# Strassen–Winograd chains of an expert layer: the second product of a chain accumulated into the first one's PSUM bank instead of added by VectorE

## The chip, the cores and the metric

One core of one Trainium2 chip. The metric is the device time of one execution in microseconds (us); less is better. Engines are called as in the profile: PE (matrix products), DVE (VectorE), ACT (ScalarE), POOL (GpSimd), SP (which issues the DMAs here).

## The reference, cut to what matters

Three stages stand one behind the other: a linear attention, a gated feed-forward layer, and a layer of eight experts, whose input `x` has 2304 tokens of 512 features. The change is in the last:

```python
logits = x @ w_gate
logits = logits - logits.max()
P = np.exp(logits)
for _ in range(8):
    P /= P.sum(1, keepdims=True) + 1e-09
    P /= P.sum(0, keepdims=True) + 1e-09
    P *= N / E
out = np.zeros((N, D), dtype=np.float32)
for e in range(E):
    h = np.maximum(x @ w1[e], 0.0)      # 512 -> 1024
    ye = h @ w2[e]                      # 1024 -> 512
    out += P[:, e:e + 1] * ye
```

## The kernel before, in words

Every float32 operand is split into a high part (H, rounded) and a low part (L, the rest), and a product is three matmuls: H·H, H·L and L·H (`mm3`, lines 86 to 88 in the profile). ACT casts the high part (L95), DVE or POOL subtracts the low part (L98).

The expert layer, which is the part from about 577 us of the span, runs over three slices `s` of 768 tokens; in each over the eight experts `e`; and in each over four **units** `p`, 96 units in all. A unit makes two of the eight 128-feature tiles of `h` for its 768 tokens, p and p+4, as one step of Strassen–Winograd: seven half-size products instead of eight, of operands that are sums of blocks. The sums of blocks of `x` (a11, a12, a22, s1 to s4) are made once for each slice, those of `w1` (B11 … T4) in the first slice for each unit: SP loads a piece of w1, ACT casts it in two pieces (768 and 1024 elements of a partition), POOL subtracts the low part of the first piece and DVE that of the second, and the result is stored; the later slices load it ready-made. Each product is 6 matmuls (two blocks of 128 rows by three) with 384 columns, 42 in a unit.

`product(x, i, *adds)` writes into one of five PSUM banks that rotate (`bufs=5`), and what is to be done with the bank stands behind it: ACT copies the first product into the SBUF tile `c` (L724), and DVE adds the others onto what lies there (L726), seven sums in a unit. With Winograd's names, the second entry c12 is a11·B11 + s2·T2, c21 is that plus s3·T3, c22 is c21 plus s1·T1, and so on: the sums hang one on the other. `h_split` (L705 to L707) then makes the two tiles of `h`: ACT the ReLU, rounded (hH), and DVE the low part (hL). Behind a unit w2 is split (`split_w2`: ACT casts 1024 elements, POOL or DVE subtracts), two units' worth of w2 rows each.

After the fourth unit of an expert follows **the py phase**: six output tiles of 128 tokens, each 24 matmuls with 512 columns that take the eight tiles of h and w2, and DVE scales and adds the result to the output tile (L834). Between products and between pairs of py matmuls, `between()` issues one step of the normalisation of P (lines 763 to 773, "Sinkhorn"), until its 16 half steps are done; until then py tiles are copied out unscaled and wait.

The order on each engine is made by the tile framework: instructions keep the program's order with priorities, `tc.high_priority(60)` puts what empties a PSUM bank ahead. The two py banks, the five product banks and the one bank of the Sinkhorn sums are used together. A new product that takes a bank waits until its last reader is done.

Of the kernel before, what the change touches and what calls it, by code (L numbers as in the profile page):

```python
# [8 lines left out]
F32 = mybir.dt.float32  # L9
# [3 lines left out]
ENG = dict(  # L13
    kh="aaav", num="a", xmul="gvgg", xh="a", xl="ggvg", woh="a",
    wol="g", w3h="a", w3l="g", w34="aaav", wh="vvvvvvav", wl="v", oh="va", ol="vvvg", Xh="a",
    Xl="v", Xs="g", Wt="v", Wh="a", Wl="gv", W2h="a", W2l="vg",
)
AF = mybir.ActivationFunctionType
ALU = mybir.AluOpType
# [3 lines left out]
def f32(ap):  # L23
    return ap.bitcast(F32)
# [3 lines left out]
def kernel(  # L28
# [17 lines left out]
    nc = tc.nc  # L46
    PSUM = bass.MemoryType.PSUM
    P = 128
# [15 lines left out]
    N1 = 384  # L64
# [13 lines left out]
    def x_at(p, kt, c0, n):  # L78
        i, o = divmod(c0, NH)
        return XHL[i][p][:, kt, o : o + n]  # L80
# [4 lines left out]
    def mm3(ps, aH, aL, bH, bL, start, stop):  # L85
        nc.tensor.matmul(ps, aH, bH, start=start, stop=False)  # L86
        nc.tensor.matmul(ps, aH, bL, start=False, stop=False)  # L87
        nc.tensor.matmul(ps, aL, bH, start=False, stop=stop)  # L88

    def engine(key, i=0):  # L90
        return {"a": nc.scalar, "v": nc.vector, "g": nc.gpsimd}[ENG[key][i % len(ENG[key])]]
# [22 lines left out]
    with ExitStack() as c1:  # L114
# [267 lines left out]
        for n in range(3 * FT):  # L382
            s = 5 * n // 3
            w, name, i = (wo_load, f"wo{n}", n) if n < FT else (w3_load, f"w3_{n - FT}", n - FT)
# [17 lines left out]
        for step in range(NB + 8):  # L402
# [5 lines left out]
            i = step - 4  # L408
# [17 lines left out]
    c4 = ctx.enter_context(ExitStack())  # L426

    NP = FT2 // 2
# [3 lines left out]
    def add(key, out, a, b, op, i=0):  # L432
        engine(key, i).tensor_tensor(out, a, b, op)
# [61 lines left out]
    def sbuf(c, name, bufs=1, side="right"):  # L495
        return c.enter_context(tc.tile_pool(name=name, bufs=bufs, side=side, reuse_waits="tile"))
# [30 lines left out]
    with ExitStack() as c2:  # L527
# [76 lines left out]
        for j in range(NT // N1):  # L604
            c0 = j * N1
            for ft in range(FT):
                ab = []
                for w in range(2):
                    n = 2 * ft + w
# [7 lines left out]
                    ps = ab_p.tile([P, N1], F32, name=f"ab{j}_{ft}_{w}", tag="ab")  # L617
# [26 lines left out]
            for dt in range(KT):  # L644
                ps = px_p.tile([P, N1], F32, name=f"px{j}_{dt}", tag="px")
# [6 lines left out]
                i, o = divmod(c0, 2 * N1)  # L652
                nc.sync.dma_start(XS[i][:, dt, o : o + N1], xt)
                xh, xl = x_at(0, dt, c0, N1), x_at(1, dt, c0, N1)
# [19 lines left out]
    with c4:  # L674
# [3 lines left out]
        sk = sbuf(c4, "sk", 2)  # L678
        st = sbuf(c4, "st", 2)
        wp = sbuf(c4, "wp")  # L680
        ph_p = c4.enter_context(tc.tile_pool(name="ph", reuse_waits="tile", bufs=5, space=PSUM))
        py_p = c4.enter_context(tc.tile_pool(name="py", reuse_waits="tile", bufs=2, space=PSUM))
        W2, rawW2 = {}, {}
        hH = [hp.tile([P, 2 * N1], F32R, name=f"hH{i}") for i in range(FT2)]
# [20 lines left out]
        def h_split(ft, src):  # L705
            nc.scalar.activation(hH[ft], src, AF.Relu)  # L706
            nc.vector.scalar_tensor_tensor(hL[ft], src, 0.0, f32(hH[ft]), ALU.max, ALU.subtract)  # L707

        def unit(u, between):
            s, e, p = units[u]  # L710
            c = ut.tile([P, 4, N1], F32, name=f"c{u}", tag="c")
            c11, c21, c12, c22 = (c[:, i] for i in range(4))
            B11, B21, B22, T1, T2, T3, T4 = range(7)

            def product(x, i, *adds):
                ps = ph_p.tile([P, N1], F32, name=f"p{x}{u}", tag="ph")
                (wh, wl), (xh, xl) = WC[u], XC[x]
                for kt in range(2):
                    k = slice(kt * P, (kt + 1) * P)
                    mm3(ps, wh[:, i, k], wl[:, i, k], xh[:, kt], xl[:, kt], kt == 0, kt == 1)  # L720
                with tc.high_priority(60):
                    for o, t in adds:
                        if t is None:
                            nc.scalar.copy(o, ps)  # L724
                        else:
                            nc.vector.tensor_tensor(o, t, ps, ALU.add)  # L726
                between()

            product("a11", B11, (c11, None))
            product("s2", T2, (c12, c11))  # L730
            product("s3", T3, (c21, c12))
            product("s1", T1, (c22, c21), (c12, c12))
            product("a12", B21, (c11, c11))
            product("a22", T4, (c21, c21))
            h_split(p, c[:, 0:2].rearrange("p a n -> p (a n)"))
            product("s4", B22, (c12, c12))
            h_split(p + NP, c[:, 2:4].rearrange("p a n -> p (a n)"))

        m1 = sk.tile([P, 1], F32, name="m1", tag="m1", bufs=1)
        m2 = sk.tile([1, 1], F32, name="m2", tag="m2", bufs=1)  # L740
# [44 lines left out]
        def between():  # L785
            if todo:
                todo.pop()()
# [3 lines left out]
        for u, (s, e, p) in enumerate(units):  # L791
# [7 lines left out]
            if u + 2 >= len(W1S):  # L799
                prep_w1(u + 2)  # L800
            unit(u, between)
            split_w2(u)
            load_w2(u + 2)
# [6 lines left out]
            for tt in range(2 * N1 // P):  # L810
                t = s * 2 * N1 // P + tt
                ps = py_p.tile([P, DM], F32, name=f"py{e}_{t}", tag="py")
# [3 lines left out]
                o = oacc[tt]  # L816
# [96 lines left out]
```

## Time and profile before

| | us |
|---|---|
| median of 3 runs | 2124.03 (2122.5 to 2124.05) |
| profiled execution, its span | 2119.5 |
| PE busy | 2064.6 (97%) |
| DVE busy | 1155.2 (55%) |
| ACT busy | 600.5 (28%) |
| POOL busy | 348.2 (16%) |

The profiled execution is one execution; its span is the time from its first to its last recorded instruction, 4.5 us below the median. Busy time is the time in which at least one recorded instruction of the engine runs. Times of rows count from the start of the span. A row of the trace has the start, the duration of one instruction, the engine, the line, and output and inputs by the program's names; in square brackets stands how long the engine idled before it, and what it then waited for. Consecutive instructions of an engine overlap a little in the records, so that the distance of two starts is the better measure of what an instruction takes of its engine.

### The profile page before, as it was taken

Reading aid. Unit: us, or ns where it says so; the run is one execution under the profiler, and the core shown is the slowest. Engines: PE = TensorE matmul, PEld = TensorE weight load, DVE = VectorE, ACT = ScalarE, POOL = GpSimd, SP = SyncE. Lnnn points to the kernel's source line nnn. Section 1 sums busy time; section 2 is a strip of 40 time slices with the busy share of each in tenths; the row PEclk is TensorE's granted clock in tenths of the full one; section 3 lists DMA queues with packets and bytes.
Section 4 is the critical chain, followed back from the end, with each engine's and each line's share of the span. In section 5 each row is a group of like instructions: output and inputs, shape, how many; then the busy total and the mean of one; then the engine's idle time right before and its main releaser. Section 6 shows DMA issues by size and latency. Waiting matters only on the chain.

```text
span 2119.5 us, 28336 instructions
## 1 busy us (share of the span) xinstructions
PE 2064.6 (97%) x11621; PEld 1843.6 (87%) x11621; DVE 1155.2 (55%) x1766; ACT 600.5 (28%) x947; POOL 348.2 (16%) x204
## 2 busy tenths in 40 slices
PE   8899889999889999999999999999999999999999
PEld 6677789999878888888888999888999888999887
DVE  8876863333486556665555554444565444555443
ACT  6665432222332222332231221111232111122111
POOL 2432221121422211221120000000010000000000
PEclk9999999999989999999999999999999999999999
DMA  6432244555474556645564443334444334444330
GB/s 210 136 128 84 103 147 139 167 174 161 159 292 150 195 218 238 231 182 188 184 243 169 179 179 135 118 130 155 179 184 170 135 108 151 177 179 166 127 120 30
DMA packets 78529, 345.40 MB, mean 163 GB/s; under 512 B 7488, under 2 KB 11456, under 8 KB 65728
## 3 DMA queue, kind: packets, MB, share of 16 engines
q1 hardware_dynamic: 77808, 342.95, 45.0%
q8 instruction: 91, 1.49, 0.3%
q10 hardware_dynamic: 592, 0.66, 0.1%
q14 instruction: 38, 0.31, 0.0%
HBM read 256.54 MB, written 87.03 MB: 162 GB/s over the span
## 4 chain that ended last, share of the span: by engine, by line
PE 82%; DVE 8%; issue 3%; DMA 2%; ACT 2%; POOL 1%; SPq 0%; ACTq 0%; DVEq 0%; POOLq 0%
PE py L88 12%; PE py L87 12%; PE py L86 12%; PE ps L86 5%; PE ps L88 5%; PE ps L87 5%; PE pa L86 4%; PE pa L88 4%; PE pa L87 4%; PE ab L88 3%; PE ab L86 3%; PE ab L87 3%; PE nu L268 1%; PE px L86 1%; PE px L87 1%
## 5 line engine op out<-in xcount | busy, mean ns | idle before, releaser
L88 PE MATMUL py<-w2h,hL 128*128 128x512 f32 x1152 | 457.2, 397 | 0.3 <-DVE hL L707 0.2
L86 PE MATMUL py<-w2h,hH 128*128 128x512 f32 x1152 | 456.8, 397 | 0.5 <-DVE o L832 0.5
L87 PE MATMUL py<-w2l,hH 128*128 128x512 f32 x1152 | 456.9, 397 | 0.0
L834 DVE SCALAR_TENSOR_TENSOR o<-py,Pw,o 128x512 f32<-128x512 f32 x126 | 94.6, 751 | 450.9 <-PE py L88 450.9
L726 DVE TENSOR_TENSOR c<-c,ps 128x384 f32<-128x384 f32 x480 | 256.1, 549 | 90.5 <-PE ps L88 84.8
L98 POOL TENSOR_TENSOR w2l<-r,w2h 128x1024 fp32r<-128x1024 f32 x48 | 116.4, 2425 | 1108.2 <-ACT w2h L95 1081.4
L95 ACT CAST w2h<-r 128x1024 fp32r<-128x1024 f32 x96 | 101.0, 1052 | 692.1 <-PE py L88 611.9
L88 PEld LDWEIGHTS py<-w2h,hL 128*128 128x128 f32 x1152 | 216.8, 188 | 55.5 <-DVE hL L707 3.3
L86 PEld LDWEIGHTS py<-w2h,hH 128*128 128x128 f32 x1152 | 217.0, 188 | 52.6 <-DVE o L832 0.8
L87 PEld LDWEIGHTS py<-w2l,hH 128*128 128x128 f32 x1152 | 217.0, 188 | 51.5
L707 DVE SCALAR_TENSOR_TENSOR hL<-c,hH 128x768 fp32r<-128x768 f32 x192 | 234.1, 1236 | 24.5 <-ACT hH L706 22.5
L706 ACT ACTIVATE hH<-c 128x768 fp32r<-128x768 f32 x192 | 158.3, 843 | 298.3 <-DVE c L726 276.3
L86 PE MATMUL ab<-XH,wH 128*128 128x384 f32 x384 | 131.5, 343 | 6.9 <-DVE wH L95 5.4
L88 PE MATMUL ab<-XH,wL 128*128 128x384 f32 x384 | 131.1, 342 | 0.6 <-DVE wL L98 0.5
L87 PE MATMUL ab<-XL,wH 128*128 128x384 f32 x384 | 130.7, 340 | 0.0
L726 DVE TENSOR_TENSOR c<-c,pa 128x384 f32<-128x384 f32 x192 | 102.4, 549 | 16.7 <-PE pa L88 15.2
L628 POOL TENSOR_TENSOR cL<-a,cH 128x384 fp32r<-128x384 f32 x48 | 58.9, 1229 | 232.2 <-ACT cH L627 232.1
L98 DVE TENSOR_TENSOR w2l<-r,w2h 128x1024 fp32r<-128x1024 f32 x48 | 59.0, 1229 | 53.8 <-ACT w2h L95 53.8
L95 ACT CAST w<-r 128x768 fp32r<-128x768 f32 x64 | 59.6, 938 | 101.0 <-DMA r<-in_moe_w_dram 30.5
L98 POOL TENSOR_TENSOR w<-r,w 128x768 fp32r<-128x768 f32 x32 | 66.6, 2082 | 130.0 <-ACT w L95 118.0
L626 DVE TENSOR_TENSOR a<-ab,a 128x384 f32<-128x384 f32 x48 | 26.7, 557 | 109.4 <-PE ab L88 109.4
L86 PEld LDWEIGHTS ab<-XH,wH 128*128 128x128 f32 x384 | 72.9, 190 | 8.3 <-DVE wH L95 4.7
(169 smaller groups left out, 3891.5 us busy)
## 6 DMA issues: line engine op xcount, KB each, us to landing
w<-w1s SPq DMA_DIRECT2D x64, 1792.0 KB, 7.6
w1s<-w SPq DMA_DIRECT2D x32, 1792.0 KB, 6.7
r<-in_moe_w_dram SPq DMA_DIRECT2D x96, 512.0 KB, 3.4
rw<-in_w_dram SPq DMA_DIRECT2D x32, 512.0 KB, 3.5
tr<-in_moe_w_dram SPq DMA_DIRECT2D x32, 512.0 KB, 4.2
w1t<-tt SPq DMA_DIRECT2D x32, 512.0 KB, 5.1
r<-w1t SPq DMA_DIRECT2D x32, 512.0 KB, 8.1
r<-in_moe_w_dram SPq DMA_DIRECT2D x32, 384.0 KB, 7.4
```

The costliest lines, as they stand in the source:

```text
L86: nc.tensor.matmul(ps, aH, bH, start=start, stop=False)
L87: nc.tensor.matmul(ps, aH, bL, start=False, stop=False)
L88: nc.tensor.matmul(ps, aL, bH, start=False, stop=stop)
L95: (e.copy if e is nc.scalar else e.tensor_copy)(out, src)
L98: engine(key, i).tensor_tensor(out, a, b, ALU.subtract)
L268: nc.tensor.matmul(o, kv[:, hh, sg, :], eq[:, sg, hh, c], start=sg == 0, stop=sg == 1)
L626: behind = nc.vector.tensor_tensor(cc, ab[1], a_sb, ALU.mult).ins
L628: nc.gpsimd.tensor_tensor(l, cc, f32(h), ALU.subtract)
L706: nc.scalar.activation(hH[ft], src, AF.Relu)
L707: nc.vector.scalar_tensor_tensor(hL[ft], src, 0.0, f32(hH[ft]), ALU.max, ALU.subtract)
L726: nc.vector.tensor_tensor(o, t, ps, ALU.add)
L834: nc.vector.scalar_tensor_tensor(o, ps, Pw[:, t, e : e + 1], o, ALU.mult, ALU.add)
```

## The change

The banks of the products are no longer five that rotate, but four with names of their own, one bank each: p16, p53, p74 and p2 (`bufs=1`, a tag for each). The order of the products is now a11 (p16), s1 (p53), s3 (p74), s2 (p16, added by PE onto a11's product, which ACT has copied to c11 before), a12 (p2), s4 (p53, onto s1's) and a22 (p74, onto s3's). ACT copies four times in a unit (`kept`, L734), DVE adds four times (`added`, L739), and POOL adds c12 to c22 in SBUF (`add("Ht", …)`, L433, 128x384). The matmuls of products stand in L726 of the new kernel. `h_split` of tile p+4 comes ahead of that of tile p. Nothing else is edited.

```diff
-        ph_p = c4.enter_context(tc.tile_pool(name="ph", reuse_waits="tile", bufs=5, space=PSUM))
+        ph_p = c4.enter_context(tc.tile_pool(name="ph", reuse_waits="tile", bufs=1, space=PSUM))
...
-            def product(x, i, *adds):
-                ps = ph_p.tile([P, N1], F32, name=f"p{x}{u}", tag="ph")
+            bank = {}
+
+            def product(k, x, i):
+                start = k not in bank
+                if start:
+                    bank[k] = ph_p.tile([P, N1], F32, name=f"{k}{u}", tag=k)
+                ps = bank[k]
...
+                        nc.tensor.matmul(
+                            ps, w[:, i, kc], m[:, kt], start=start and kt == n == 0,
+                            stop=kt == 1 and n == 2, skip_group_check=True,
+                        )
...
-            product("a11", B11, (c11, None))
-            product("s2", T2, (c12, c11))
-            product("s3", T3, (c21, c12))
-            product("s1", T1, (c22, c21), (c12, c12))
-            product("a12", B21, (c11, c11))
-            product("a22", T4, (c21, c21))
+            kept(c11, product("p16", "a11", B11))
+            kept(c22, product("p53", "s1", T1))
+            kept(c12, product("p74", "s3", T3))
+            add("Ht", c22, c22, c12, ALU.add)
+            u2 = product("p16", "s2", T2)
+            kept(c21, u2)
+            added(c11, c11, product("p2", "a12", B21))
+            between()
+            added(c22, c22, u2)
+            added(c12, c21, product("p53", "s4", B22))
+            between()
+            h_split(p + NP, c[:, 2:4].rearrange("p a n -> p (a n)"))
+            added(c21, c21, product("p74", "a22", T4))
+            between()
             h_split(p, c[:, 0:2].rearrange("p a n -> p (a n)"))
-            product("s4", B22, (c12, c12))
-            h_split(p + NP, c[:, 2:4].rearrange("p a n -> p (a n)"))
```

What this does to the order of three engines. In the rows below a name's number is that of the tile; w_26 is the w1 piece of unit 26.

DVE in the first slice, between the sums of unit 24 and those of unit 25 (the first and second unit of an expert), before:

```order
L707 SCALAR_TENSOR_TENSOR hL_5672<-c_8619,hH_5664 128x768
L726 TENSOR_TENSOR c_8696<-c_8696,ps_8705 128x384
L707 SCALAR_TENSOR_TENSOR hL_5676<-c_8619,hH_5668 128x768
L726 TENSOR_TENSOR c_8696<-c_8696,ps_8713 128x384
L98 TENSOR_TENSOR w_26_8687<-r_26_8616,w_26_8687 128x1024
L726 TENSOR_TENSOR c_8696<-c_8696,ps_8721 128x384 x2
L726 TENSOR_TENSOR c_8696<-c_8696,pa_8730 128x384
L726 TENSOR_TENSOR c_8696<-c_8696,pa_8738 128x384
L726 TENSOR_TENSOR c_8696<-c_8696,ps_8748 128x384
```

and with the change, with the numbers of units in the names (p1625 is bank p16 of unit 25):

```order
L707 SCALAR_TENSOR_TENSOR hL4_5676<-c24_8571,hH4_5668 128x768
L707 SCALAR_TENSOR_TENSOR hL0_5672<-c24_8571,hH0_5664 128x768
L98 TENSOR_TENSOR w1_26_8637<-r1_26_8568,w1_26_8637 128x1024
L739 TENSOR_TENSOR c25_8646<-c25_8646,p1625_8647 128x384
L739 TENSOR_TENSOR c25_8646<-c25_8646,p225_8679 128x384
L739 TENSOR_TENSOR c25_8646<-c25_8646,p5325_8655 128x384
L739 TENSOR_TENSOR c25_8646<-c25_8646,p7425_8663 128x384
```

The first two sums of the next unit stood between the two hL and the w1 subtraction; now both hL and the subtraction stand ahead of all four, and the first sum is the one that frees p16.

POOL around the same place, before:

```order
L98 TENSOR_TENSOR w_25_8610<-r_25_8383,w_25_8610 128x768
L98 TENSOR_TENSOR w2l_8759<-r_25_8452,w2h_8758 128x1024
L98 TENSOR_TENSOR w2l_8913<-r_27_8762,w2h_8912 128x1024
L98 TENSOR_TENSOR w_26_8687<-r_26_8616,w_26_8687 128x768
L98 TENSOR_TENSOR w_27_8764<-r_27_8693,w_27_8764 128x768
```

and with the change:

```order
L98 TENSOR_TENSOR w2l_8707<-r_25_8404,w2h_8706 128x1024
L433 TENSOR_TENSOR c_8571<-c_8571 128x384
L98 TENSOR_TENSOR w2l_8857<-r_27_8710,w2h_8856 128x1024
L98 TENSOR_TENSOR w_26_8637<-r_26_8568,w_26_8637 128x768
L433 TENSOR_TENSOR c_8646<-c_8646 128x384
L98 TENSOR_TENSOR w_27_8712<-r_27_8643,w_27_8712 128x768
```

POOL's new addition of a unit (c_8571 is unit 24's, c_8646 unit 25's) stands behind w2 and w1 subtractions that belong to other units.

PE at the end of the gated layer, where the logits of the last tokens (`lg`, then `lp`) and the first expert's first product meet, before:

```order
L590 MATMUL lg_5618<-XH_69,WG 16x384
L591 MATMUL lg_5618<-XL_70,WG 16x384
L595 MATMUL lp<-ident,lgs_5627 128x16 x3
L86 MATMUL pa_5696<-a11h_5460,w_0_5492 128x384
L87 MATMUL pa_5696<-a11l_5461,w_0_5492 128x384
```

and with the change, behind the matmuls of the products a11, s1 and s3:

```order
L726 MATMUL p_5696<-s2h_5470,w_0_5492 128x384
L726 MATMUL p_5696<-s2l_5471,w_0_5492 128x384
L726 MATMUL p_5696<-s2h_5470,w_0_5492 128x384 x2
L726 MATMUL p_5696<-s2l_5471,w_0_5492 128x384
L726 MATMUL p_5696<-s2h_5470,w_0_5492 128x384
L726 MATMUL p_5746<-a12h_5479,w_0_5492 128x384
L726 MATMUL p_5746<-a12l_5480,w_0_5492 128x384
L726 MATMUL p_5746<-a12h_5479,w_0_5492 128x384
L590 MATMUL lg_5618<-XH_69,WG 16x384
```

27 matmuls of products (four products of six, and three of a12) now stand ahead of the last L590 of the logits. Farther on, the third py tile stands behind 220 matmuls of products and 48 of py, where it stood behind 249 and 48.

## Rows read from the trace of the kernel before

**Rows 1.** The page, its first part: busy time of each engine.
```profile
PE 2064.6 (97%) x11621; PEld 1843.6 (87%) x11621; DVE 1155.2 (55%) x1766; ACT 600.5 (28%) x947; POOL 348.2 (16%) x204
```

**Rows 2.** Busy time by stretch: first slice from its third expert, the later slices.
```profile
core 0: us, PE busy (x) PEld busy (x) DVE busy (x) ACT busy (x) POOL busy (x), PEclk, DMA share, GB/s
...
727.30:1109.30 382.00, 380.39 (x1874) 336.59 (x1873) 223.22 (x293) 116.42 (x148) 81.68 (x38) 1.00 0.57 209
1109.30:2115.60 1006.30, 1006.26 (x4993) 900.03 (x4991) 489.47 (x711) 200.08 (x262) 81.17 (x34) 1.00 0.40 147
```

**Rows 3.** Timeline of PE, first matmuls of units: start us, duration us, engine, line.
```profile
727.30 0.33 PE L86 MATMUL pa<-a11h,w 128*128 128x384 f32 x1
...
918.60 0.34 PE L86 MATMUL pa<-a11h,w 128*128 128x384 f32 x1
...
925.91 0.33 PE L86 MATMUL pa<-a11h,w 128*128 128x384 f32 x1
...
933.19 0.33 PE L86 MATMUL pa<-a11h,w 128*128 128x384 f32 x1
...
940.83 0.33 PE L86 MATMUL pa<-a11h,w 128*128 128x384 f32 x1
...
1109.27 0.34 PE L86 MATMUL pa<-a11h,w 128*128 128x384 f32 x1
...
2052.51 0.34 PE L86 MATMUL pa<-a11h,w 128*128 128x384 f32 x1
```

**Rows 4.** Groups of instructions by line: count | busy us, mean ns of one.
```profile
L726 DVE TENSOR_TENSOR c<-c,ps 128x384 f32<-128x384 f32 x480 | 256.1, 549 | 90.5 <-PE ps L88 84.8
...
L98 POOL TENSOR_TENSOR w<-r,w 128x768 fp32r<-128x768 f32 x32 | 66.6, 2082 | 130.0 <-ACT w L95 118.0 <-DVE c L726 6.3 <-DMA r<-in_moe_w_dram 5.7
...
L98 DVE TENSOR_TENSOR w<-r,w 128x1024 fp32r<-128x1024 f32 x32 | 40.4, 1262 | 17.7 <-ACT w L95 17.6
```

**Rows 5.** The gated layer's POOL subtraction: duration ns, least/median/most.
```profile
L628 POOL TENSOR_TENSOR cL<-a,cH x48: 1006/1024/5785, 258.5 to 559.4; 128x384 fp32r<-128x384 f32 x48
```

**Rows 6.** Timelines of ACT, POOL and DVE behind an expert's first unit.
```profile
924.93 1.05 ACT L95 CAST w2h<-r 128x1024 fp32r<-128x1024 f32 x1 [2.89 <-DMA r<-in_moe_w_dram]
925.88 0.85 ACT L706 ACTIVATE hH<-c 128x768 fp32r<-128x768 f32 x1
926.63 0.81 ACT L95 CAST w<-r 128x768 fp32r<-128x768 f32 x1
927.35 0.47 ACT L724 COPY c<-pa 128x384 f32<-128x384 f32 x1
927.72 0.85 ACT L706 ACTIVATE hH<-c 128x768 fp32r<-128x768 f32 x1
...
926.06 2.41 POOL L98 TENSOR_TENSOR w2l<-r,w2h 128x1024 fp32r<-128x1024 f32 x1 [4.43 <-ACT w2h L95]
928.42 2.57 POOL L98 TENSOR_TENSOR w<-r,w 128x768 fp32r<-128x768 f32 x1
...
926.76 2.52 DVE L707 SCALAR_TENSOR_TENSOR hL<-c,hH 128x768 fp32r<-128x768 f32 x1
929.20 0.54 DVE L726 TENSOR_TENSOR c<-c,ps 128x384 f32<-128x384 f32 x1
929.67 2.13 DVE L707 SCALAR_TENSOR_TENSOR hL<-c,hH 128x768 fp32r<-128x768 f32 x1
```

**Rows 7.** Timeline of PE where the expert layer starts.
```profile
585.87 0.50 PE L590 MATMUL lg<-XH,WG 128*16 128x384 f32 x1 [8.56 <-ACT XH L655]
...
588.03 0.69 PE L86 MATMUL pa<-a11h,w 128*128 128x384 f32 x1
...
599.72 0.29 PE L770 MATMUL cs<-Pw,ones 128*128 128x144 f32 x1
...
643.92 0.36 PE L770 MATMUL cs<-Pw,ones 128*128 128x144 f32 x1
...
649.18 0.36 PE L770 MATMUL cs<-Pw,ones 128*128 128x144 f32 x1
...
654.82 0.50 PE L86 MATMUL py<-w2h,hH 128*128 128x512 f32 x1 [0.47 <-DVE o L832]
```

## What the change will do to the time, forecast before it was run

> **What bounds the kernel now.** I read the page's first part first. PE is busy for 97% of the span, DVE for 55%, ACT and POOL far less [rows 1], so a change that touches DVE, ACT and POOL can gain only where PE waits for one of them. Where that is, the view of busy time by stretch tells: in the two later slices PE is busy for 1006.26 of 1006.30 us, in the first slice, from its third expert on, for 380.39 of 382.00 [rows 2]. The timeline of PE sharpens it. Sixteen experts less the last lie between 1109.27 and 2052.51, so one takes 943.24 / 15 = 62.88 us; an undisturbed unit takes 933.19 - 925.91 = 7.28, and what is left for the py phase is 62.88 - 4 x 7.28 = 33.76 [rows 3]. That is PE's own pace: 7.28 / 42 = 0.173 us for a matmul of a product and 33.76 / 144 = 0.234 for one of py. The six experts from 727.30 to 1109.27 take 63.66 each, 0.78 more; 0.36 of that is in the third unit (940.83 - 933.19 = 7.64) [rows 3], the rest in py. So in the first slice the chain of other engines' work, which there includes the split of w1, already touches PE's pace, and in the later ones nothing does. The third place is the start of the expert layer, where PE idles 8.56 us for the last logits, and the Sinkhorn steps then decide when the third py tile may start [rows 7].
>
> **What is removed, and what it is worth.** Three of seven DVE sums a unit go: 3 x 549 ns, 1.65 us of a unit of 7.28 [rows 4]. PE's matmuls stay 42 a unit, since the additions on a bank cost no matmul of their own. In the later slices DVE is busy for 489 of 1006 us [rows 2]; the sums lie beside PE's work, and their removal is worth nothing there.
>
> **What is added.** Three ACT copies a unit (starts 0.37 us apart, 927.72 - 927.35 [rows 6]) and one POOL addition of 384 elements of a partition in SBUF. That addition has no row before; the nearest is POOL's subtraction of the same size, 1.01 us at least and 5.79 at most [rows 5]. I take 1.0 and keep the upper end for the rivals.
>
> **The later slices: zero.** The banks now have fixed owners, so each one's next use may wait. By PE's pace, s2 ends at 4.16 us of a unit, its copy and its sum (0.37 and 0.55) by about 5.4, and p16 is wanted again at 7.28: 1.9 us to spare. For p53 s4 ends at 6.24, its sum at 6.9, and it is wanted at 8.32; for p74 it is 7.28, 7.9 and 9.36: 1.4 us each. What covers these is that nothing else long is on DVE then; were the cover gone, PE would wait by what is missing, in all 64 units.
>
> **The first slice.** Here the split of w1 stands between. The rows show that long DVE and POOL instructions on SBUF data exclude one another, and the first to come goes first: hL at 926.76 takes 2.52 us and ends at 929.28, 0.81 after POOL's w2 subtraction (928.47); POOL's next one starts at 928.42 and takes 2.57, ending 1.71 after hL; and the next hL (929.67, 2.13) again ends 0.81 after that. The sum from PSUM between them takes its ordinary 0.54 [rows 6]. The Trainium skill (Perfetto Trace Analysis, Optimizing Scalar/DVE Operations) says that GPSIMD and DVE share an SBUF read port and that moving work between the two might not help; the trace agrees, hL 2.52 instead of some 0.8, and by that rule too POOL's new addition costs DVE what it takes.
>
> In the new order both hL and the w1 subtraction of DVE stand ahead of all four sums of the next unit, and the first of these, onto c22, also needs POOL's addition and frees p16. I walk that through in us from an expert's first matmul (918.60), with what one takes from [rows 6]: ACT's starts 0.95 apart for a cast of 1024, 0.75 for hH, 0.72 for the cast of 768, 0.37 for a copy; hL 0.81 to 0.9, POOL's w1 piece 1.7 to 1.8, DVE's w1 piece 1.1 (1.26 in the mean, which holds waits [rows 4]), a sum 0.47 to 0.55. The w2 cast comes at 6.33 (924.93, as its DMA lands) and ends at 7.38. Then ACT: hH to 8.1, cast to 8.85, copy of c11, hH to 9.95, copy of c22, cast to 11.3, copy of c12 to 11.65. POOL subtracts w2 from 7.4 to 9.8; the first hL is held and ends at 10.65; POOL's w1 piece follows to 12.35, the second hL to 13.2, POOL's addition to 14.2, DVE's w1 piece to 15.3, and the first sum of the second unit to 15.8. The third unit wants p16 at 14.56. **PE waits 1.25 us.** Queued behind the late sum on DVE are the other three sums, which free p2, p53 and p74, and with them hH, and the next hL.
>
> After that the ring of one unit is hL 0.9 + POOL's w1 piece 1.8 + hL 0.9 + addition 1.0 + DVE's w1 1.1 + four sums 1.9 + 0.35 until hH is there = 7.95 us, 0.67 over PE's 7.28. With the sum that frees p16 the fourth unit starts 0.8 late again: it starts at 23.95 instead of 21.84, so the units lose 2.1. One ring more brings the last hL to 37.15. The first py tile wants it at 31.2 + 18 x 0.234 + 0.5 = 35.9, so py loses 1.25. Together **3.3 us an expert, where 0.78 is lost now: 2.5 more.** The last expert of the slice splits w1 in two units only, so the 0.8 of its fourth unit falls away: 1.7 more. In the second expert half of the units' 2.1 counts, 1.1, as PE waits for Sinkhorn there in any case; the first has no earlier unit to carry. Sum: 5 x 2.5 + 1.7 + 1.1 = +15.4. The bounds: nothing, if the ring stays under 7.28, and about +31, if POOL's addition takes twice as much in this crowd.
>
> **The start.** 27 product matmuls move into the wait of 8.56 us, and the third py tile has 29 fewer product matmuls ahead of it (220 for 249), which are left for later: 29 x 0.173 = 5.0 us more behind it. When can it start? Before, at 654.82, which is 5.64 after the last of eight Sinkhorn sums; seven distances between these fill 599.72 to 649.18, 7.07 each, and the last is 5.26 [rows 7]. If the distances stay at 7.07, nothing moves and the change costs 5.0. If all are 5.26, the tile starts 12.7 earlier, and it gains 7.6. With three DVE sums fewer between the steps I take 5.8: 8.9 earlier, **-3.8** net.
>
> **Sum.** 15.4 - 3.8 = +11.6. The profiled execution would have a span of 2119.5 + 11.6 = 2131.1; the median stands 4.5 above that execution, so 2135.6.
>
> **Rivals.**
> Faster: the ring is shorter than PE's unit. If POOL's w1 piece (1.8 of the 7.95) ran beside the four sums, which pass POOL unharmed [rows 6], the ring would be 6.15 and the first slice would lose even its 0.78 x 6 = 4.7 of now; with the start's -3.8 it gives 2115.5. The point is whether ACT's cast of 768 ends before DVE's first hL begins. For it speaks that DVE has 1.65 us less to do; against it that the cast stands behind hH in ACT's order, and that hH releases hL too. I give it 0.17.
>
> No difference: the ring fits, but the first stall of each expert remains in part, as the w2 subtraction of POOL comes at the same time whatever the ring does. Half a microsecond more for seven experts, 3.5, and -3.8 from the start: 2123.7. For it speaks that before, with an equally long list, the third unit lost only 0.36 [rows 3]. I give it 0.18.
>
> Much slower: the four single banks hold PE in every unit, in the later slices too. At 0.3 us a unit it is 64 x 0.3 = 19 more, 2155. The spare 1.4 to 1.9 us speak against it; 0.07. The Trainium skill (Perfetto Trace Analysis, Matmuls) asks that independent groups of matmuls rotate through different PSUM banks, so that the emptying of one overlaps the next; by it this change is the wrong way round. No row before shows the banks as the limit.
>
> The clock is one more price in the slower cases: right behind the idle 8.56 us a product's matmul takes 0.69 in its row and not 0.33 [rows 3, 7]; were PE to idle that long again, it would count twice. The stalls above are of one microsecond, so I count nothing for it. That the change doesn't do what it says can be left out: the order has four sums and 42 matmuls in a unit.
>
> **How the numbers follow.** The forecast, slower by more than 0.2% (4.2 us, about what a measurement of this kernel can tell from no change), gets 0.58, with its own range from 2128 to 2150 (the start's bounds, and the stalls at about half and at one and a half of their size). With the rivals: slower 0.58 + 0.07 = 0.65, same 0.18, faster 0.17. The range leaves out the much slower case and the better part of the faster one, 0.07 + 0.12: 2117 to 2150.
>
> **What would show it.** Right, if the six middle experts of the first slice take some 66 us instead of 63.66, if the late matmul there is the first of the third and fourth units and waits for the sum onto c22 behind DVE's w1 piece, if the last hL holds the first py tile, and if the sixteen later experts stay at 62.88. In the start the distances of the Sinkhorn sums should be near 5.8. Wrong, if the units of the first slice take 7.28 with POOL's addition in place, or if a later slice's unit takes more than 7.28.

## The result, and the profile after

The changed kernel takes 2145.98 us (median of 4 runs, 2141.11 to 2147.45), the kernel before 2124.04 (4 runs, 2122.5 to 2125.57): a ratio of 1.0101, 95% interval 1.0087 to 1.0115, 22 us slower. The forecast was 2135.6 in a range of 2117 to 2150.

The first part of the page and the groups of DVE, ACT and POOL in the changed kernel, which answer to [rows 1, 4, 5]:

```profile
PE 2072.8 (97%) x11621; PEld 1846.7 (86%) x11621; DVE 1037.7 (48%) x1478; ACT 728.4 (34%) x1235; POOL 479.9 (22%) x300
...
L739 DVE TENSOR_TENSOR c<-c,p 128x384 f32<-128x384 f32 x384 | 200.0, 550 | 163.4 <-POOL c L433 116.2
...
L707 DVE SCALAR_TENSOR_TENSOR hL<-c,hH 128x768 fp32r<-128x768 f32 x192 | 240.8, 1265 | 29.6 <-ACT hH L706 27.4
L706 ACT ACTIVATE hH<-c 128x768 fp32r<-128x768 f32 x192 | 160.6, 845 | 211.4 <-DVE c L739 195.3
L734 ACT COPY c<-p 128x384 f32<-128x384 f32 x384 | 181.0, 478 | 119.6 <-PE p L726 119.0
L433 POOL TENSOR_TENSOR c<-c 128x384 f32<-128x384 f32 x96 | 132.8, 1384 | 272.9 <-ACT c L734 272.9
```

DVE is busy for 118 us less and the kernel is 22 us slower. The sums now wait: of their 163 us of idle time before them 116 end with POOL's new addition, which takes 1.38 us in the mean.

The timeline of PE in the changed kernel: the logits matmul ahead of the wait, the third py tile, first matmuls of experts and of late units, two late py matmuls, and the first matmul of the last expert:

```profile
580.99 0.35 PE L591 MATMUL lg<-XL,WG 128*16 128x384 f32 x1
...
650.27 0.50 PE L86 MATMUL py<-w2h,hH 128*128 128x512 f32 x1
...
730.96 0.34 PE L726 MATMUL p<-a11h,w 128*128 128x384 f32 x1
...
945.37 0.44 PE L726 MATMUL p<-a11h,w 128*128 128x384 f32 x1 [1.00 <-DVE c L739]
953.29 0.44 PE L726 MATMUL p<-a11h,w 128*128 128x384 f32 x1 [0.34 <-DVE c L739]
966.54 0.50 PE L88 MATMUL py<-w2h,hL 128*128 128x512 f32 x1 [0.99 <-DVE hL L707]
...
1061.59 0.34 PE L726 MATMUL p<-a11h,w 128*128 128x384 f32 x1
1132.65 0.34 PE L726 MATMUL p<-a11h,w 128*128 128x384 f32 x1
1609.33 0.50 PE L88 MATMUL py<-w2h,hL 128*128 128x512 f32 x1 [2.40 <-DVE hL L707]
...
2078.66 0.34 PE L726 MATMUL p<-a11h,w 128*128 128x384 f32 x1
```

In the kernel before, the matmul that answers to the first of these, and the first matmul of the eighth expert, which answers to the one at 1061.59:

```profile
576.96 0.35 PE L591 MATMUL lg<-XL,WG 128*16 128x384 f32 x1
...
1045.61 0.34 PE L86 MATMUL pa<-a11h,w 128*128 128x384 f32 x1
```

**Where the 26.2 us between the two profiled executions (2145.7 and 2119.5) lie.** The logits matmul stands 4.0 later already (580.99 against 576.96), by code that the change does not touch, so that is one execution against another; 22.2 are the change's, which is what the medians show. From there to the third expert it is -0.4 (730.96 - 727.30 = 3.66, less 4.03). The five experts from there to the eighth take 330.63 instead of 318.31: +12.3. The eighth, the last of the first slice, takes 71.06 instead of 63.66: +7.4. The sixteen later ones, by the distance of 1132.65 to the last expert's start at 2078.66 (946.0 for 943.2), lose 2.8, which is the wait at 1609.33, at the second change of slice. That is 22.1.

The windows of the same two stretches as [rows 2]:

```profile
730.96:1132.65 401.69, 386.57 (x1873) 340.27 (x1872) 205.11 (x221) 143.63 (x220) 124.66 (x62) 0.99 0.54 199
1132.65:2142.00 1009.35, 1006.66 (x4993) 899.98 (x4991) 393.68 (x519) 290.78 (x454) 161.69 (x98) 1.00 0.40 147
```

PE waits 15.1 us in the first slice's six experts, where it waited 1.6, and in the later slices 2.7, at one place. Inside a unit the lateness runs as in the forecast. DVE and POOL in the changed kernel behind the first unit of the expert at 929.65:

```profile
937.92 4.98 DVE L707 SCALAR_TENSOR_TENSOR hL<-c,hH 128x768 fp32r<-128x768 f32 x2 [0.24 <-ACT hH L706]
942.83 2.03 DVE L98 TENSOR_TENSOR w<-r,w 128x1024 fp32r<-128x1024 f32 x1
944.78 2.12 DVE L739 TENSOR_TENSOR c<-c,p 128x384 f32<-128x384 f32 x4
...
937.15 2.41 POOL L98 TENSOR_TENSOR w2l<-r,w2h 128x1024 fp32r<-128x1024 f32 x1 [1.66 <-PE p L726]
939.52 2.57 POOL L98 TENSOR_TENSOR w<-r,w 128x768 fp32r<-128x768 f32 x1
942.04 1.73 POOL L433 TENSOR_TENSOR c<-c 128x384 f32<-128x384 f32 x1
```

The two hL take 4.98 us together, because POOL's w2 and w1 subtractions stand between them; the w1 subtraction of DVE takes 2.03 beside POOL's addition; the first sum ends at 945.3, and PE's third unit starts at 945.37.

### The profile page after: what moved, and what is told of

It reads as the page before. It is cut to its first block, busy times and chain, and to the rows that moved or that the text cites. A ratio compares the mean times of both kernels' runs of the same rounds, so it can differ in the third digit from the quotient of the medians.

```text
span 2145.7 us, 28206 instructions
## 1 busy us (share of the span) xinstructions
PE 2072.8 (97%) x11621; PEld 1846.7 (86%) x11621; DVE 1037.7 (48%) x1478; ACT 728.4 (34%) x1235; POOL 479.9 (22%) x300
## 4 chain that ended last, share of the span: by engine, by line
PE 73%; DVE 9%; issue 8%; ACT 4%; POOL 4%; DMA 3%; SPq 0%; ACTq 0%; POOLq 0%; DVEq 0%
PE p L726 23%; PE py L88 11%; PE py L86 11%; PE py L87 11%; PE ab L88 3%; PE ab L86 3%; PE ab L87 3%; DMA r<-in_moe_w_dram 2%; DVE hL L707 1%; PE nu L268 1%; PE px L88 1%; PE px L87 1%; PE px L86 1%; POOL c L433 1%; PE pp L164 1%
## 5 line engine op out<-in xcount | busy, mean ns | idle before, releaser
L739 DVE TENSOR_TENSOR c<-c,p 128x384 f32<-128x384 f32 x384 | 200.0, 550 | 163.4 <-POOL c L433 116.2
L707 DVE SCALAR_TENSOR_TENSOR hL<-c,hH 128x768 fp32r<-128x768 f32 x192 | 240.8, 1265 | 29.6 <-ACT hH L706 27.4
L734 ACT COPY c<-p 128x384 f32<-128x384 f32 x384 | 181.0, 478 | 119.6 <-PE p L726 119.0
L433 POOL TENSOR_TENSOR c<-c 128x384 f32<-128x384 f32 x96 | 132.8, 1384 | 272.9 <-ACT c L734 272.9
L726 PE MATMUL p<-a11h,w 128*128 128x384 f32 x384 | 115.0, 340 | 10.3 <-DVE c L739 10.3
L726 PE MATMUL p<-s1h,w 128*128 128x384 f32 x384 | 114.0, 337 | 0.7 <-DVE c L739 0.7
L726 PE MATMUL p<-s4h,w 128*128 128x384 f32 x384 | 113.9, 337 | 0.0
L726 PE MATMUL p<-s3h,w 128*128 128x384 f32 x384 | 113.7, 336 | 0.0
```

Source lines behind the costliest of these rows:

```text
L726: nc.tensor.matmul(ps, w[:, i, kc], m[:, kt], start=start and kt == n == 0, stop=kt == 1 and n == 2, skip_group_check=True,)
```

## The experiments

**The addition on DVE** (`ht_dve`).

```diff
-    ..., Ht="g",
+    ..., Ht="v",
```

> Only the engine of the addition c22 += c12 is changed, from POOL to DVE; it still reads two SBUF operands. Theory A (POOL's addition shuts out DVE and is shut out by it, in the chain to the sum that frees p16): about 0.5 us on DVE takes the place of 1.0 us on POOL in the ring of the first slice, 7.95 becomes 7.45, so the late starts of the third and fourth unit fall from 1.1 and 0.5 us to under half, and the time by 8 to 14 us, to 2132 to 2138. Theory B (four single banks are too few, whoever adds): the same stalls, 2144 to 2148. Theory C (ACT's three more copies make everything late): 2144 to 2148 too.

2140.32 us, ratio 1.0079 (1.0062 to 1.0096): 5.7 us less than the change, in the direction of theory A but short of its 8 to 14. The stretch of six experts, PE's wait for the third unit, and the two engines ahead of it:

```profile
730.89:1124.64 393.75, 384.21 (x1874) 338.63 (x1872) 212.54 (x245) 143.08 (x220) 82.00 (x38) 0.99 0.56 203
...
940.88 0.44 PE L726 MATMUL p<-a11h,w 128*128 128x384 f32 x1 [1.10 <-DVE c L739]
...
934.92 2.57 POOL L98 TENSOR_TENSOR w<-r,w 128x768 fp32r<-128x768 f32 x1
...
933.26 5.04 DVE L707 SCALAR_TENSOR_TENSOR hL<-c,hH 128x768 fp32r<-128x768 f32 x2 [0.16 <-ACT hH L706]
```

The fourth unit's wait and most of the py wait are gone, the third unit's is not: the two hL still take 5.04 us between POOL's w2 and w1 work. So the addition is a part of the ring, and not what holds the first one.

**The sum straight from bank p74** (`sum_psum`).

```diff
-            kept(c12, product("p74", "s3", T3))
-            add("Ht", c22, c22, c12, ALU.add)
+            added(c22, c22, product("p74", "s3", T3))
+            between()
```

> The addition in SBUF and ACT's copy of s3's product are left out; DVE adds s3's product to c22 straight from bank p74 (five sums from PSUM a unit, three copies, no POOL). Theory A: no addition on the shared port is left, the ring of the first slice is 7.95 - 1.0 + 0.5 = 7.45 at most and less where the sum passes POOL's work; units of the first slice near 7.28 to 7.5, slice changes free of their 2.5 us, 2118 to 2128. Theory B: banks as before it, 2140 to 2148. Theory C: one of three added copies gone, 2138 to 2142.

2134.29 us, ratio 1.0046 (1.0029 to 1.0063): 11.7 less than the change and outside the range of A, between A and B. The six experts take 390.91:

```profile
729.47:1120.38 390.91, 382.84 (x1873) 336.52 (x1872) 211.21 (x245) 134.11 (x196) 81.71 (x38) 1.00 0.56 205
```

POOL's 82 us of w1 and w2 work are the same as in the run before, and half the loss is still there.

**Bank p16 doubled** (`two_p16`).

```diff
-                    bank[k] = ph_p.tile([P, N1], F32, name=f"{k}{u}", tag=k)
+                    bank[k] = ph_p.tile([P, N1], F32, name=f"{k}{u}", tag=k, bufs=2 if k == "p16" else 1)
```

> Bank p16 doubled (five product banks again), all else as in the change. Theory A: the chain of sums is late as a whole, so PE then waits for p53 (wanted 1.04 us after p16, summed 0.9 later) and the last hL of an expert still comes 1.2 us late: 2141 to 2148. Theory B: the stalls at the first product of a unit vanish, 2124 to 2132.

2151.67 us, ratio 1.013 (1.0115 to 1.0145): above even A's range, and B falls. The wait only goes to the next bank, s1's p53:

```profile
950.12 0.44 PE L726 MATMUL p<-s1h,w 128*128 128x384 f32 x1 [0.87 <-DVE c L739]
958.04 0.44 PE L726 MATMUL p<-s1h,w 128*128 128x384 f32 x1 [0.34 <-DVE c L739]
970.35 0.50 PE L88 MATMUL py<-w2h,hL 128*128 128x512 f32 x1 [1.12 <-DVE hL L707]
```

Its six middle experts take 401.03 us, no more than the change's 401.69; the 5.7 us that it is slower by lie at the start. Its first matmul of a product comes at 588.20, 13.5 us after the last px matmul, as in the kernel before (13.6), which also has five product banks; in the change it comes 2.7 us after. By the start of the third expert `two_p16` is 7.1 us behind the change, counted from the last px matmul of each. Why the fifth bank holds the first products back was not tested.

**Both w1 subtractions on DVE** (`w1_dve`).

```diff
-    ..., Wl="gv", ...
+    ..., Wl="v", ...
```

> Both pieces of w1's low part are subtracted by DVE; POOL keeps the new addition and its half of w2. Theory A: POOL's 1.8 us leaves the ring and 0.85 us of DVE comes in, 7.95 becomes 7.0, under PE's 7.28: the fourth unit starts on time, the last hL too, and only the third unit is late where POOL has w2: 2128 to 2136. Theory B: 2144 to 2148. Theory C: 2144 to 2148.

2123.44 us, ratio 0.9997 (0.9987 to 1.0006, 10 runs): 22.5 less than the change, more than A expected; B and C fall. DVE gets more work and the kernel is faster. What is left of the ring (one turn of the second and third unit):

```profile
719.18:1108.35 389.17, 383.95 (x1873) 337.75 (x1872) 202.54 (x243) 143.22 (x220) 75.70 (x40) 1.00 0.56 206
...
931.67 1.67 POOL L433 TENSOR_TENSOR c<-c 128x384 f32<-128x384 f32 x1 [6.98 <-ACT c L734]
...
933.37 2.14 DVE L739 TENSOR_TENSOR c<-c,p 128x384 f32<-128x384 f32 x4 [0.90 <-POOL c L433]
```

Its units take 7.69 and not the 7.0 of the expectation: POOL's addition is held by DVE and then holds the sums for 0.9 us a turn.

**The same move in the kernel before** (`before_w1_dve`), the same edit of one letter.

> The kernel before with both w1 subtractions on DVE, which took 22 us off the changed kernel. Theory A (the exclusion of DVE and POOL costs where the order has no spare time behind it; before, five rotating banks and sums between the two hL carried it): little is there to gain, its units lose 0.36 us only, and DVE makes three sums more: 2118 to 2126. Rival D (POOL's w1 piece is simply a bad place, in either kernel): the kernel before gains as much, 2102 to 2110.

2114.98 us, ratio 0.996 (0.9945 to 0.9975): 8.4 less than before: 3 under A's range and 5 above D's, so neither held as written. POOL's w1 piece costs the kernel before 8, and the changed one 22.

**All of w2 on DVE** (`w2_dve`).

```diff
-    ..., W2l="vg", ...
+    ..., W2l="v", ...
```

> The change with all w2 low parts on DVE; POOL keeps w1's first piece and the addition. Theory A: an expert's first ring loses POOL's 2.4 us of w2, so its third unit starts on time (7.3 to 7.5 instead of 8.3 to 8.45), while the fourth unit, behind the ring of 7.95, stays at 7.9 or takes what the third lost (up to 8.3): 2135 to 2142. Theory B' (the addition on POOL alone holds the third unit): third unit as before it, 2143 to 2148.

2137.68 us, ratio 1.0065 (1.005 to 1.008): in A's range. The fourth unit's first matmul still waits, the third's is nearly on time:

```profile
934.60 0.44 PE L726 MATMUL p<-a11h,w 128*128 128x384 f32 x1
...
942.52 0.44 PE L726 MATMUL p<-a11h,w 128*128 128x384 f32 x1 [0.34 <-DVE c L739]
```

In this expert the third unit starts 7.53 after the second and the fourth 7.92 after the third, 8.44 and 7.92 in the change. The first wait is the w2 subtraction's, the second the ring's, as expected.

**w1 on DVE and the sum from PSUM** (`w1_psum`), the edits of `w1_dve` and `sum_psum` together.

> Two edits together: c22's addition taken from bank p74 by DVE (no copy, no POOL), and both w1 subtractions on DVE; POOL keeps half of w2. Theory A: no ring over 7.28 is left, first-slice experts 62.9 to 63.3 instead of 66 and instead of 64.0 with w1 alone; the two slice changes still lose some 2 and 4; with the start's gain of about 5 us 2113 to 2120. Rival B (single banks hold what remains): experts near 64, 2121 to 2126.

2112.22 us, ratio 0.9949 (0.9932 to 0.9965), a little under the range; six experts in 381.25 us, 0.75 less than before. B falls here a second time: the four banks are as in the change.

**The sums of blocks of x on DVE** (`x_dve`).

```diff
-    ..., Xs="g", ...
+    ..., Xs="v", ...
```

> The change with one edit: the sums of blocks of x (made once a slice) on DVE; the w1 and w2 parts and the new addition stay on POOL. Theory A (exclusion of DVE and POOL, here at the start and at the two slice changes): the slice changes lose 1 to 3 us each instead of 4.6 and 2.8, the idle stretch of PE before the last logits gets shorter, the middle experts stay at 66: 2132 to 2140. Rival E (DVE's own list ahead of the last hL is what is late at a slice change): 2143 to 2149, the slice changes as in the change.

2130.49 us, ratio 1.0034 (1.0021 to 1.0047): 15.5 less than the change, more than A expected; E falls. The middle experts stay at 66, as expected. The last expert of the first slice takes 65.53 (71.06 in the change), the one ahead of the second change of slice 62.94 (65.65), and at the start the last logits matmul goes on without the long wait:

```profile
578.43 0.35 PE L590 MATMUL lg<-XH,WG 128*16 128x384 f32 x1
...
579.02 0.35 PE L591 MATMUL lg<-XL,WG 128*16 128x384 f32 x1
```

In the change the same step came at 589.68, and before at 585.87 [rows 7]. What held it is in the changed kernel's ACT timeline: a cast waits 3.40 us for POOL's sum, and the copies of the last px tiles stand behind it on ACT. The last copy then waits for a store (`xs<-xt`) of an earlier one, which was issued at 577.46 and landed at 588.53; in `x_dve`, where two of the last four copies come ahead of the cast and not one, the store that its last copy waits for had landed at 571.99. The kernel before has the same two waits (3.40 and 8.86 us), so they are old.

```profile
575.81 0.84 ACT L95 CAST s4h<-xs 128x768 fp32r<-128x768 f32 x1 [3.40 <-POOL xs L433]
...
576.96 0.47 ACT L651 COPY xt<-px 128x384 f32<-128x384 f32 x1
...
588.61 0.48 ACT L651 COPY xt<-px 128x384 f32<-128x384 f32 x1 [3.61 <-DMA xs<-xt]
```

From the last px matmul to the third expert it is 146.6 us, 152.5 in the change: with the two changes of slice (5.5 and 2.7) these 5.9 make up 14 of the 15.5.

**The change as it was made, with w1, w2 and the x sums on DVE** (`change_w12x`): three settings, nothing else.

> The change as it was made, with its addition on POOL and its four copies, and only the w1 and w2 parts and the sums of x moved to DVE: POOL has nothing but the addition. Theory A: the ring without POOL's w1 piece is about 7.0, PE's own pace in the first slice but for 0 to 0.4 us an expert: 2100 to 2108. Theory B'' (the addition on POOL costs the chain its 1.0 us and its exclusion wherever it stands): experts of the first slice 64 and more, 2108 to 2118.

2104.01 us, ratio 0.991 (0.9895 to 0.9924), 42 less than the change. Six experts in 380.19 us, 63.4 each: near PE's pace, with the copies, the four banks and POOL's addition all in place. That ends B and C: what made the change slower is neither the banks nor ACT's copies.

**The kernel before with the same three settings** (`before_w12x`).

> The kernel before with w1, w2 and the sums of x on DVE, that is the three engine moves of the fastest kernel so far without anything of the change. Theory A (the change's sums and banks are sound, POOL beside them is not; seven DVE sums a unit beside all the splits are too much for DVE): 2104 to 2112, 4 to 12 slower than 2099.8. Rival D (the engine moves are the whole gain, the change is worth nothing): 2098 to 2102.

2104.08 us, ratio 0.9911 (0.9897 to 0.9926), at the lower end of A's range and 2 above D's. With POOL's old work out of the way the change as made is worth nothing, 2104.0 against 2104.1. That is a small gain and a small loss: from the last px matmul to the fourth expert it takes 199.6 us where this kernel takes 201.4, and its experts in the rest of the first slice take 63.3 to 63.8 where this kernel's take 62.89.

**The sum from PSUM and all three moves** (`w12x_psum`): POOL has no work left in the expert layer.

> The same, and also w2's low parts and the sums of blocks of x on DVE: POOL has no work left in the expert layer. Theory A: the slice changes lose their POOL part too, if DVE can carry it: 2108 to 2116. Rival E (at the slice change DVE's own list ahead of the last hL is too long, whoever else works): the slice changes lose 2 to 5 us as in the change, 2113 to 2122.

2099.81 us, ratio 0.989 (0.9875 to 0.9905), below the ranges of both A and E, and the fastest kernel, 1.1% under the one before. PE's stretch of six experts, and the group of hL:

```profile
712.25:1089.57 377.32, 377.32 (x1874) 337.63 (x1872) 211.70 (x283) 137.28 (x196) 0.00 (x0) 1.00 0.57 212
...
L707 DVE SCALAR_TENSOR_TENSOR hL<-c,hH 128x768 fp32r<-128x768 f32 x192 | 183.1, 954 | 9.7 <-ACT hH L706 6.7
```

PE is busy for all of the 377.32 us, 62.89 an expert, and an hL takes 0.954 us instead of 1.265. Its runs (2098.38 to 2101.66) don't overlap those of `before_w12x` (2102.84 to 2105.99), though these were runs of two sets, beside the same kernel before (2123.42 and 2123.39); so the change, with the sum taken from PSUM, is worth some 4 us, once POOL is out of the way. They lie at the start: from the last px matmul to the fourth expert it takes 197.7 us, `before_w12x` 201.4, and from there both run at PE's pace.

## Why the prediction was right, and where it was short

**The bound and the place.** Right: the later slices' units stay at 7.28, and the experts there at 62.89 but for the one ahead of the second change of slice (65.65); the loss is in the first slice.

**The walk through the ring.** Right, term by term, from the fourth to the seventh expert. Forecast were 1.25 us for the third unit, 0.8 for the fourth and 1.25 for py. In the expert at 929.65 the units' starts stand 8.44 and 7.92 apart, 1.16 and 0.64 over 7.28, and its last unit and py take 42.39, 1.38 over the 41.01 of an undisturbed one; the releasers are the ones named, the sums and hL. The 0.64 is what the ring's own terms give (7.95 - 7.28 = 0.67); the 0.8 of the forecast's sum is a little more than they add up to. In the third expert the waits are spread otherwise: its units' starts stand 9.25 and 8.99 apart, and py is 0.3 late. The five experts from the third to the seventh were to lose 12.5 more than before and lost 12.3. The Trainium skill (SBUF — State Buffer, Who interferes with whom) says that a DVE instruction with two SBUF inputs contends with a GpSimd instruction that reads SBUF, that the port pair they share is an exclusive lock and the order of issue decides who blocks, and that a DVE instruction with one SBUF input, outside the modes that use two ports, is free of it. The traces agree: hL with 4.98 us for two, against 0.954 each where POOL has no work, and the sums with one input from PSUM at 0.55.

**The cause.** The forecast put it on POOL's addition and on the order that puts both hL and the w1 subtraction ahead of the sum that frees p16. The runs show DVE and POOL in each other's way as the cause, and the addition as its smaller part: moved to DVE it gave 5.7, taken from PSUM 11.7, while w1's subtraction alone gave 22.5 and the x sums 15.5. For w1 and w2 it is the exclusion itself, since hL does not read what POOL makes there; for the x sums ACT's casts also wait for POOL's results, and the runs don't part the two. All of that is old work on POOL; w1's piece cost the kernel before only 8.4. Without the three of them the change costs nothing. That the order is what makes the same POOL work dearer fits these numbers, but the order was not put back by itself, so that much is argued. The number of banks is the less likely reason: a fifth one, for p16, left the middle experts as they were.

**The start: -3.8 forecast.** Right by its own terms: the third py tile comes at 650.27 - 4.03 = 646.24 instead of 654.82, 8.6 earlier (8.9 was forecast), and 5.0 us of matmuls are left behind it, -3.6. Two errors nearly cancel in that: the seven distances of the Sinkhorn sums are 6.1 in the mean and not 5.8, and the tile follows the last sum by 3.6 us, where the forecast left the 5.6 of before. But the second expert, for which half of the units' loss was taken (1.1) and none of py's, lost the whole: from the start to the third expert only -0.4 came out, so it lost some 3.2. PE waits in it 2.10 us for a sum (at 688.56) and 0.99 for hL (at 701.81).

**The last expert of a slice: 1.7 forecast, 7.4 measured, and nothing forecast for the second change of slice, 2.8 measured.** Here a step failed. The forecast said of the later slices that nothing else long is on DVE then, and has no term for the split of the next slice's x, which POOL, ACT and DVE make at a change of slice. In the new order a part of it stands ahead of both last hL. DVE, POOL and ACT in the changed kernel ahead of the wait at 1609.33:

```profile
1603.85 0.96 DVE L98 TENSOR_TENSOR s2l<-xs,s2h 128x768 fp32r<-128x768 f32 x1 [1.22 <-ACT s2h L95]
1604.73 0.55 DVE L739 TENSOR_TENSOR c<-c,p 128x384 f32<-128x384 f32 x1
1605.19 2.35 DVE L98 TENSOR_TENSOR a12l<-rx,a12h 128x768 fp32r<-128x768 f32 x1
1607.47 1.81 DVE L707 SCALAR_TENSOR_TENSOR hL<-c,hH 128x768 fp32r<-128x768 f32 x2
...
1604.89 1.84 POOL L433 TENSOR_TENSOR xs<-rx,xs 128x768 f32<-128x768 f32 x1 [1.94 <-DVE s2l L98]
...
1602.98 0.84 ACT L95 CAST s2h<-xs 128x768 fp32r<-128x768 f32 x1 [2.03 <-POOL xs L433]
```

s2l waits for a cast that waits for POOL's sum, a12l takes 2.35 us beside the next of POOL's sums, and both stand ahead of the two hL for which PE waits 2.40 us. In the kernel before, where PE does not wait, DVE comes to one hL ahead of a12l and to both ahead of s2l:

```profile
1579.72 2.36 DVE L707 SCALAR_TENSOR_TENSOR hL<-c,hH 128x768 fp32r<-128x768 f32 x1
1582.01 0.94 DVE L98 TENSOR_TENSOR a12l<-rx,a12h 128x768 fp32r<-128x768 f32 x1
1582.88 0.94 DVE L707 SCALAR_TENSOR_TENSOR hL<-c,hH 128x768 fp32r<-128x768 f32 x1
1583.75 0.94 DVE L98 TENSOR_TENSOR s2l<-xs,s2h 128x768 fp32r<-128x768 f32 x1
```

With the x sums on DVE the wait is gone (`x_dve`). At the first change of slice PE's wait of 2.38 us was followed by a stretch at the lower clock level, which accounts for as much again (below); the forecast had counted nothing for the clock, since its stalls were of one microsecond. And the fourth unit of that expert, whose wait was to fall away, started 0.63 late all the same.

**The sum.** 11.6 was forecast and 22 measured: 8.5 of the 10.4 missing are the two changes of slice, some 2 the second expert. That the time lies within the range owes something to luck: the upper end stood for longer stalls in every expert, and these came out as forecast; what was missing came from places that had no term or half of one.

**The rivals.** The faster one asked whether ACT's cast of 768 ends before DVE's first hL begins; it does not (the cast ends at 938.6 in the expert at 929.65, hL begins at 937.92). The second, that the ring fits and only each expert's first stall remains, falls with the fourth unit's 7.92; its reason, 0.36 us in the third unit before, was read from one expert, and in the six it lies between 0.25 and 1.19. The third, banks that hold PE in every unit, falls with the later slices' 7.28 and with `change_w12x`. The rule on rotating banks that the prediction sets beside it from the Trainium skill (Perfetto Trace Analysis, Matmuls) finds no case here: four banks of fixed use and five that rotate take 2104.0 and 2104.1 us.

## What to carry to other kernels

A change that takes work off a busy engine can lose by what it gives to another: before moving an elementwise instruction with SBUF inputs to POOL, look at which DVE instructions with two SBUF inputs run beside POOL, and how much longer they are there than alone. Where a walk through a ring gives more than PE's pace, walk it also where the ring meets other work (here the change of slice), since that is where the same cause cost the most. And when a change is slower, try the old work on the same resource as well as the new: three settings that the change had not touched made 42 us here, on a change that had lost 22.

## What was not expected of the hardware

After PE's wait at the first change of slice (2.38 us idle, then a matmul at 1100.70) the windows of the changed kernel show the granted clock at 0.50, the lower of the two levels, and after the one at the second (2.40 us idle) at 1.00:

```profile
1100.70 0.80 PE L88 MATMUL py<-w2h,hL 128*128 128x512 f32 x1 [2.38 <-DVE hL L707]
...
1101.20:1106.80 5.60, 5.60 (x14) 4.29 (x14) 1.94 (x3) 0.00 (x0) 0.00 (x0) 0.50 0.46 142
1609.40:1614.00 4.60, 4.60 (x20) 3.73 (x21) 2.28 (x3) 0.00 (x0) 0.00 (x0) 1.00 0.15 57
```

At 0.50 the 14 matmuls took 0.43 us each instead of 0.234, some 2.7 us in all, as much as the wait itself. What tells the two places apart the runs don't show. The first had another wait 3 us ahead of it (0.57 us idle, up to 1097.59), but that is not needed for it: in `ht_dve` PE idles 2.39 us at the first change of slice with no other wait above 0.1 us in that py phase, and the clock stands at 0.50 behind it too, while in `sum_psum` it stays at 1.00 there behind 2.27 us.

The stage ahead of the changed code, which is the same in both kernels, differs by 4 us between the two profiled executions (580.99 against 576.96). The difference of two profiles is to be read from the first point at which the kernels differ, not from the start.
